# Layer change of a two-layer gated network: tile 2's parts taken from the PSUM banks, second products one block later, s*q+b on VectorE

## The chip, the cores and the metric

The kernel runs on one core of one Trainium2 chip. The metric is the device time of one execution in microseconds, median of three runs. Each core has TensorE (PE, matmuls, with the queue PEld for its weight loads), VectorE (DVE), ScalarE (ACT), GpSimd (POOL) and SyncE (SP, which issues the loads here).

## The reference

A retention layer gives 1536 tokens of 512 values. Two dense layers with 2048 hidden units follow. The change concerns the passage from the first to the second.

```python
def _moe_ref(x, w_in, w_out):          # first layer
    h = x @ w_in
    g = np.maximum(h, 0.0) + np.log1p(np.exp(-np.abs(h)))
    return (g @ w_out).astype(np.float32)

def _moe2_ref(x, w_in, w_out, s, b):   # second layer
    h = x @ w_in
    r = np.maximum(h, 0.0)
    g = s * (r * r) + b
    return (g @ w_out).astype(np.float32)
```

## The kernel before

**Tiles.** The 1536 tokens are three tiles of 512 (`j` = 0, 1, 2), the 512 values four chunks of 128 (`cc`). The activations of a tile stand in `xa[j]` as plain fp32 and, for the matmuls, as two parts: `xh` (rounded) and `xl` (what is left). A product with two parts on each side takes three matmuls, high by high, high by low, low by high, so a block of four chunks takes 12 matmuls of 512 columns. Weights are split in the same way: one 64-bit weight tile `raw` is turned into fp32 by two VectorE operations into `word` (L290, L292), a ScalarE copy into `wm` (L295) and a third VectorE operation (L300), and then into `wh` (ScalarE) and `wl` (GpSimd) by `split`, L110. `split_w` is a generator of these steps, and `go(work, n)` runs n of them.

**A block.** A first product gives a bank of hidden values: `h`, `y` or `third`. The activation function turns it into `c`, and `parts_g` splits `c` into `gh` (ScalarE) and `gl` (GpSimd). In the second layer the function is Relu (L559), Square (L584), and s*q+b as a ScalarE Identity with scale and bias (L585). The second products then add `gh`, `gl` times `w_out` into four sum banks (`acc01`, two banks in one tile, `acc2`, `acc3`); there is one set of them, so whoever comes next must wait until they are emptied into `xa` (`take_2`: in the first pair of the second layer a VectorE copy, L621; later an addition, L623).

**The change of layer.** The last steps of the first layer end with tile 2: `end` runs the second products of step `NS - 1`, `sum_last` adds the banks to `xa[2]` (L423), and `parts_last` makes `xh` (ScalarE, L428) and `xl` (VectorE, L430) of it. Meanwhile `plain(1, 0, ...)` runs the first pair of hidden blocks of the second layer: six blocks, `k` = 0 to 5, two for each tile. With each block goes an entry of `accs`: three of the old layer (`left`), then the two second products of tile 0 (`whole`), then nothing. From pair 1 on, `second` uses a scheme with fewer products, in which sums of the tiles (`sum_x` with x1 to x4, `sum_z`) replace the tiles; their sums and parts are made in the same stretch.

**What sets the order.** The order is written by hand: the code is issued as it stands, each engine works off its own queue in that order, and waits are set where one engine needs another's result. Between two engines there is no other order.

Of the kernel before, what the change touches and what calls it, by code (L numbers as in the profile page):

```python
# [7 lines left out]
F32 = mybir.dt.float32  # L8
F32R = mybir.dt.float32r
U32 = mybir.dt.uint32  # L10
AF = mybir.ActivationFunctionType
ALU = mybir.AluOpType
# [10 lines left out]
NTILE = NT // TT  # L23
CPT = TT // C
KC = DM // P
# [23 lines left out]
def tile_retention_mlps(ctx: ExitStack, tc: tile.TileContext, head, w1, w2, sb, out):  # L49
    nc = tc.nc  # L50
# [31 lines left out]
    sbt = cp.tile([P, 2], F32, tag="sbt", name="sbt")  # L82
# [335 lines left out]
    def sum_last(banks):  # L418

        la, g, j, _ = steps[NS - 1]  # L420
        for cc in banks:
            t = xa[j][:, cc]
            nc.vector.tensor_tensor(out=t, in0=acc_t[la, g, j][cc], in1=t, op=ALU.add)  # L423

    def parts_last():
        j = NTILE - 1
        for cc in range(KC):
            nc.scalar.activation(xh[j][:, cc], xa[j][:, cc], AF.Copy)  # L428
        for cc in range(KC):
            nc.vector.tensor_tensor(  # L430
                out=xl[j][:, cc], in0=xa[j][:, cc], in1=xh[j][:, cc].bitcast(F32), op=ALU.subtract
            )

    x_t, x3 = {}, {}

# [119 lines left out]
    def begin(la, src, own=False, by_pool=True, tags=None):  # L555

        if la:
            c = src if own else next_t()
            nc.scalar.activation(c, src, AF.Relu)  # L559
            return src, c, None  # L560
        if tags:
            r, u = (late.tile([P, TT], F32, tag=tag, name=tag) for tag in tags)
        else:
            r, u = next_t(), None
        if by_pool:
            nc.scalar.activation(r, src, AF.Relu)
            return src, r, u if tags else src if own else next_t()
        nc.vector.tensor_scalar(
            out=r.bitcast(U32), in0=src.bitcast(U32), scalar1=0x80000000, scalar2=None, op0=ALU.bitwise_or
        )  # L570
        nc.scalar.activation(r, r, AF.Softplus)
        return src, r, None

    def middle(of):

        src, r, u = of
        if u is not None:
            nc.vector.scalar_tensor_tensor(out=u, in0=r, scalar=-2.0, in1=src, op0=ALU.mult, op1=ALU.add)
            nc.scalar.activation(u, u, AF.Softplus)

    def finish(la, p, half, j, of):
        src, c, u = of
        if la:
            nc.scalar.activation(c, c, AF.Square)  # L584
            nc.scalar.activation(c, c, AF.Identity, scale=sbt[:, 0:1], bias=sbt[:, 1:2])  # L585
        elif u is not None:
            nc.gpsimd.tensor_tensor(out=c, in0=c, in1=u, op=ALU.add)  # L587
            late_parts.append((la, p, half, j, c))
            return
        else:  # L590
            nc.vector.scalar_tensor_tensor(out=c, in0=src, scalar=0.0, in1=c, op0=ALU.max, op1=ALU.add)
        parts_g(la, p, half, j, c)
# [3 lines left out]
    def parts_g(la, p, half, j, c):  # L596
        gg_t[la, p, half, j] = gh, gl = next_g()
        split(gh, gl, c, nc.scalar, nc.gpsimd)
# [29 lines left out]
    NS = len(steps)  # L628
# [54 lines left out]
    def go(work, n):  # L683
        for _ in range(n):
            next(work, None)
# [68 lines left out]
    with tc.manual_schedule():  # L754
# [149 lines left out]
        def end_part():  # L904
            while late_parts:
                parts_g(*late_parts.pop(0))
            go(late_work, 1)
# [34 lines left out]
        def of_pair(la, p, j, half):  # L942
            def take(banks):
                if half:
                    take_2(la, p, j, banks)

            return lambda banks: acc_2(la, p, j, half, banks), take

        def whole(acc, take):
            acc(FIRST + SECOND)  # L950
            take(FIRST + SECOND)

        def plain(la, p, left, sums, parts):

            w = la * NF + 2 * p
            base = at[la, p + 1]
            accs = left + [lambda: whole(*of_pair(la, p, 0, 0)), lambda: whole(*of_pair(la, p, 0, 1)), lambda: None]
            banks = [(ps_h, "h"), (ps_y, "y"), None, (ps_h, "h"), None, (ps_y, "y")]
            for k, (j, half) in enumerate((j, half) for j in range(NTILE) for half in range(2)):
                part(base + k + 2 if la or k > 1 else 0)  # L960
                to = bank(*banks[k]) if banks[k] else bank_2[1]
                all_of(to, w_t[w + half, 0], j)
                if la and k == 2:
                    end_part()
                    accs[k]()
                of = begin(la, to, by_pool=False)
                if not la:
                    end_part()
                    go(work, 2)
                finish(la, p, half, j, of)  # L970
                if la:
                    end_part()
                if not la or k != 2:
                    accs[k]()
                go(work, 3 if la else 1)
                for x in sums[k]:
                    next(x, None)
                for x in parts[k]:
                    parts_x(x, la)
# [286 lines left out]
```

## Time and profile before

| | us |
|---|---|
| median of three runs | 565.93 (565.83 to 566.22) |
| the profiled execution | 565.88 |
| its span | 564.0 |
| TensorE busy | 557.2 (99%) |
| VectorE busy | 383.7 (68%) |
| ScalarE busy | 349.4 (62%) |
| GpSimd busy | 348.9 (62%) |

Times of rows are microseconds from the span's start. A row of windows holds a stretch and its length, the busy time and (in brackets) the number of instructions of PE, PEld, DVE, ACT and POOL in this order, TensorE's granted clock as a share of full speed (1.00 is 2.4 GHz), the busy share of the DMA engines and GB/s. A matmul's record is 0.39 us long, but the next one starts 0.227 us later: the records overlap, so busy time hides gaps shorter than the overlap, and a wait is read from the starts. The same holds on ScalarE and VectorE, where one operation starts a little before the record of the one before it ends.

### The profile page before, as it was taken

How to read it: one execution, taken by the hardware profiler on the slowest of the kernel's cores; microseconds unless marked ns; L12 is line 12 of the kernel's file. 1: busy time of each engine (PE TensorE's matmuls, PEld its weight loads, DVE VectorE, ACT ScalarE, POOL GpSimd, SP SyncE). 2: the span in 40 equal slices, each digit the busy share in tenths (PEclk: the TensorE clock that was granted, in tenths of full speed). 3: DMA queues.
4: the chain of work that ended last, by engine and by line, in shares of the span. 5: the costliest groups of instructions: out<-in, count | busy, mean ns of one | idle time of the engine just before them, and what ended most of it. 6: DMA issues, size and time to landing. Idle time of an engine off the chain costs nothing.

```text
span 564.0 us, 8397 instructions
## 1 busy us (share of the span) xinstructions
PE 557.2 (99%) x3098; PEld 465.4 (83%) x3098; DVE 383.7 (68%) x581; ACT 349.4 (62%) x641; POOL 348.9 (62%) x293
## 2 busy tenths in 40 slices
PE   8999999999999999999999999999999999999997
PEld 7877888888888888888888777888888888888886
DVE  4887768776757759786859887675665665656334
ACT  3766673544554665543437878858687776868561
POOL 4457467776598797733525999647566555646230
PEclk9999999999999999999999999999999999999999
DMA  8986112101222213322212022222211221110005
GB/s 342 405 355 223 41 38 65 48 29 48 74 76 73 76 37 111 115 76 77 73 38 76 0 74 76 76 74 76 75 63 53 74 74 41 73 38 2 0 11 213
DMA packets 15016, 50.61 MB, mean 90 GB/s; under 512 B 1792, under 2 KB 2048, under 8 KB 14976
## 3 DMA queue, kind: packets, MB, share of 16 engines
q1 hardware_dynamic: 14976, 50.08, 25.1%
q8 instruction: 24, 0.39, 0.3%
q14 instruction: 16, 0.13, 0.1%
HBM read 46.93 MB, written 3.15 MB: 89 GB/s over the span
## 4 chain that ended last, share of the span: by engine, by line
PE 92%; POOL 4%; ACT 2%; DVE 1%; issue 1%; DVEq 0%
PE acc L613 33%; PE acc L403 11%; PE h L494 9%; PE y L494 8%; PE h L352 8%; PE third L494 5%; PE y L352 4%; PE y L502 3%; PE third L502 2%; PE y L191 2%; PE s L172 2%; PE h L502 1%; PE h L191 1%; POOL gl L115 1%; PE acc L775 1%
## 5 line engine op out<-in xcount | busy, mean ns | idle before, releaser
L115 POOL TENSOR_TENSOR wl<-wm,wh 128x512 fp32r<-128x512 f32 x64 | 84.6, 1322 | 101.0 <-ACT wh L112 101.0
L115 POOL TENSOR_TENSOR gl<-c,gh 128x512 fp32r<-128x512 f32 x69 | 91.0, 1324 | 70.3 <-ACT gh L112 48.5
L623 DVE TENSOR_TENSOR xa<-acc,xa 128x512 f32<-128x512 f32 x131 | 82.3, 683 | 71.4 <-PE acc L613 71.2
L613 PE MATMUL acc<-wh,gl 128*128 128x512 f32 x190 | 74.3, 391 | 0.0
L613 PE MATMUL acc<-wh,gh 128*128 128x512 f32 x190 | 74.1, 390 | 0.0
L613 PE MATMUL acc<-wl,gh 128*128 128x512 f32 x190 | 53.9, 390 | 0.0
L112 ACT ACTIVATE gh<-c 128x512 fp32r<-128x512 f32 x69 | 43.6, 632 | 10.9 <-POOL c L587 6.9
L295 ACT ACTIVATE wm<-raw 128x512 f32<-128x512 f32 x64 | 42.4, 663 | 8.7 <-POOL wl L115 8.6
L300 DVE SCALAR_TENSOR_TENSOR wm<-wm,cu,word 128x512 uint32<-128x512 uint32 x54 | 39.9, 739 | 4.1 <-ACT wm L295 3.4
L292 DVE SCALAR_TENSOR_TENSOR word<-raw,cu,word 128x512 uint32<-128x512 uint32 x54 | 40.8, 756 | 1.9
L613 PEld LDWEIGHTS acc<-wl,gh 128*128 128x128 f32 x190 | 35.7, 188 | 7.6
L112 ACT ACTIVATE wh<-wm 128x512 fp32r<-128x512 f32 x64 | 39.7, 620 | 3.2 <-DVE wm L300 3.0
L613 PEld LDWEIGHTS acc<-wh,gl 128*128 128x128 f32 x190 | 35.8, 188 | 6.6
L613 PEld LDWEIGHTS acc<-wh,gh 128*128 128x128 f32 x190 | 35.8, 188 | 6.4
L585 ACT ACTIVATE c<-c,sbt 128x512 f32<-128x512 f32 x48 | 39.2, 816 | 1.6
L365 ACT ACTIVATE t<-t 128x512 f32<-128x512 f32 x24 | 15.1, 629 | 38.9 <-DVE t L359 38.9
L403 PE MATMUL acc<-gh,wh 128*128 128x512 f32 x96 | 37.9, 395 | 0.0
L403 PE MATMUL acc<-gl,wh 128*128 128x512 f32 x96 | 37.4, 390 | 0.0
L613 PE MATMUL acc<-gh,wh 128*128 128x512 f32 x96 | 37.3, 389 | 0.0
L613 PE MATMUL acc<-gl,wh 128*128 128x512 f32 x96 | 37.3, 389 | 0.0
L290 DVE TENSOR_SCALAR word<-raw 128x512 uint32<-128x512 uint32 x54 | 37.0, 686 | 0.4
L559 ACT ACTIVATE c<-c 128x512 f32<-128x512 f32 x21 | 13.1, 633 | 33.6 <-DVE c L552 33.6
(265 smaller groups left out, 1461.4 us busy)
## 6 DMA issues: line engine op xcount, KB each, us to landing
raw<-w SPq DMA_DIRECT2D x64, 512.0 KB, 3.5
qk<-head SPq DMA_DIRECT2D x12, 512.0 KB, 8.3
kv<-head SPq DMA_DIRECT2D x12, 512.0 KB, 8.4
out<-xa SPq DMA_DIRECT2D x11, 256.0 KB, 2.1
cst<-head SPq DMA_DIRECT2D x1, 518.0 KB, 4.4
cst<-head SPq DMA_DIRECT2D x1, 256.0 KB, 5.4
out<-xa SPq DMA_DIRECT2D x2, 128.0 KB, 1.8
sbt<-sb SPq DMA_DIRECT2D x1, 1.0 KB, 10.3
```

The lines of the kernel that those rows point to most:

```text
L112: nc.scalar.activation(hi, src, AF.Copy)
L115: lo_eng.tensor_tensor(out=lo, in0=src, in1=hi.bitcast(F32), op=ALU.subtract)
L290: nc.vector.tensor_scalar(out=x, in0=lw, scalar1=29, scalar2=None, op0=ALU.logical_shift_right)
L292: nc.vector.scalar_tensor_tensor(out=x, in0=hw, scalar=cu[:, 0:1], in1=x, op0=ALU.bitwise_and, op1=ALU.bitwise_or)
L295: nc.scalar.activation(m, hw.bitcast(F32), AF.Copy, scale=REBIAS)
L300: nc.vector.scalar_tensor_tensor(out=m.bitcast(U32), in0=m.bitcast(U32), scalar=cu[:, 1:2], in1=x, op0=ALU.logical_shift_left, op1=ALU.bit ...
L352: nc.tensor.matmul(ps, w[:, cc * P : (cc + 1) * P], r[j][:, cc, :], start=i == 0, stop=i == len(ops) - 1)
L403: nc.tensor.matmul(acc_t[la, g, j][cc], *ops[i], start=f4 == 0 and i == 0, stop=ends(s) and i == 2)
L494: nc.tensor.matmul(ps, w[a][:, k * P : (k + 1) * P], x[b][:, k], start=start and i == 0, stop=i == len(ops) - 1, skip_group_check=True,)
L585: nc.scalar.activation(c, c, AF.Identity, scale=sbt[:, 0:1], bias=sbt[:, 1:2])
L613: nc.tensor.matmul(acc_t[la, p, "pair", j][cc], *ops[i], start=half == 0 and i == 0, stop=half == 1 and i == 2)
L623: nc.vector.tensor_tensor(out=dst, in0=ps, in1=dst, op=ALU.add)
```

## The change

Four things change, all at the change of layer, and nothing else in the program.

- `sum_last` adds `xa[2]` into the sum banks and leaves the result there; `parts_last` reads the banks, ScalarE for `xh`, VectorE for `xl`; a new `whole_last` copies the banks to `xa[2]` on ScalarE (four copies), after the Relu of block `k` = 2.
- In the second layer's first pair `accs` is now: three of the old layer, nothing, and then the two second products of tile 0. They go with blocks 4 and 5 instead of 3 and 4. The banks of blocks 4 and 5 are exchanged: block 4 goes to `y` and block 5 to `third`.
- In blocks 2 to 5 a new `squared` makes the Square on ScalarE and s*q+b as a VectorE tensor-scalar operation, both in place on `c`.
- In these blocks two steps of the weights (L290, L292 with the ScalarE copy, L300) come between `squared` and `parts_g`, so `gh` follows them.

```diff
         for cc in banks:
-            t = xa[j][:, cc]
-            nc.vector.tensor_tensor(out=t, in0=acc_t[la, g, j][cc], in1=t, op=ALU.add)
+            t = acc_t[la, g, j][cc]
+            nc.vector.tensor_tensor(out=t, in0=t, in1=xa[j][:, cc], op=ALU.add)
...
+        ps = acc_t[la, g, j]
         for cc in range(KC):
-            nc.scalar.activation(xh[j][:, cc], xa[j][:, cc], AF.Copy)
+            nc.scalar.activation(xh[j][:, cc], ps[cc], AF.Copy)
...
+            nc.vector.tensor_tensor(out=xl[j][:, cc], in0=ps[cc], in1=xh[j][:, cc].bitcast(F32), op=ALU.subtract)
+
+    def whole_last():
+        la, g, j, _ = steps[NS - 1]
+        for cc in range(KC):
+            nc.scalar.activation(xa[j][:, cc], acc_t[la, g, j][cc], AF.Copy)
...
+    def squared(c):
+        nc.scalar.activation(c, c, AF.Square)
+        nc.vector.tensor_scalar(
+            out=c, in0=c, scalar1=sbt[:, 0:1], scalar2=sbt[:, 1:2], op0=ALU.mult, op1=ALU.add
+        )
...
-            accs = left + [lambda: whole(*of_pair(la, p, 0, 0)), lambda: whole(*of_pair(la, p, 0, 1)), lambda: None]
+            own_accs = [lambda: whole(*of_pair(la, p, 0, 0)), lambda: whole(*of_pair(la, p, 0, 1))]
+            accs = left + ([lambda: None] + own_accs if la else own_accs + [lambda: None])
             banks = [(ps_h, "h"), (ps_y, "y"), None, (ps_h, "h"), None, (ps_y, "y")]
+            if la:
+                banks[4:] = banks[:3:-1]
...
                 of = begin(la, to, by_pool=False)
+                if la and k == 2:
+                    whole_last()
                 if not la:
                     end_part()
                     go(work, 2)
-                finish(la, p, half, j, of)
-                if la:
+                if la and k > 1:
+                    squared(of[1])
                     end_part()
+                    go(work, 2)
+                    parts_g(la, p, half, j, of[1])
+                    go(work, 1)
+                else:
+                    finish(la, p, half, j, of)
+                if la and k < 2:
+                    end_part()
+                    go(work, 3)
                 if not la or k != 2:
                     accs[k]()
-                go(work, 3 if la else 1)
+                if not la:
+                    go(work, 1)
```

What this does to the queues, at three places. VectorE from the last subtraction for `xl` on, before (`word` and `wm` are the weights' steps, `xa1<-xa0,xa1` is the sum for x4, `xa0<-acc` empties the sum banks, `xa2<-xa2` are the sums for z):

```order
L430 TENSOR_TENSOR xl2_108<-xa2_111,xh2_105 128x512 x4
L290 TENSOR_SCALAR word_1170<-raw_2878 128x512
L292 SCALAR_TENSOR_TENSOR word_1170<-raw_2878,cu_99,word_1170 128x512
L300 SCALAR_TENSOR_TENSOR wm_3226<-wm_3226,cu_99,word_1170 128x512
L448 TENSOR_TENSOR xa1_110<-xa0_109,xa1_110 128x1024
L621 COPY xa0_109<-acc01_3209 128x512 x2
L621 COPY xa0_109<-acc2_3210 128x512
L621 COPY xa0_109<-acc3_3211 128x512
L290 TENSOR_SCALAR word_1170<-raw_3005 128x512
L292 SCALAR_TENSOR_TENSOR word_1170<-raw_3005,cu_99,word_1170 128x512
L300 SCALAR_TENSOR_TENSOR wm_3279<-wm_3279,cu_99,word_1170 128x512
L538 TENSOR_TENSOR xa2_111<-xa2_111 128x2x256 x2
```

And of the change, from the sum for x4 on (the two first s*q+b and the first three weight operations stand ahead of it):

```order
L452 TENSOR_TENSOR xa1_110<-xa0_109,xa1_110 128x1024
L587 TENSOR_SCALAR c_3241<-c_3241,sbt_98 128x512
L290 TENSOR_SCALAR word_1170<-raw_3005 128x512
L292 SCALAR_TENSOR_TENSOR word_1170<-raw_3005,cu_99,word_1170 128x512
L300 SCALAR_TENSOR_TENSOR wm_3249<-wm_3249,cu_99,word_1170 128x512
L542 TENSOR_TENSOR xa2_111<-xa2_111 128x2x256 x2
L587 TENSOR_SCALAR c_3289<-c_3289,sbt_98 128x512
L290 TENSOR_SCALAR word_1170<-raw_3062 128x512
L292 SCALAR_TENSOR_TENSOR word_1170<-raw_3062,cu_99,word_1170 128x512
L300 SCALAR_TENSOR_TENSOR wm_3297<-wm_3297,cu_99,word_1170 128x512
L631 COPY xa0_109<-acc01_3260 128x512 x2
L631 COPY xa0_109<-acc2_3261 128x512
```

The copies that empty the sum banks move from just behind the sum for x4 to behind two s*q+b, two groups of weight operations and the sums for z.

ScalarE from the Relu of block 3 on, before (`c<-h` is that Relu, `x4h` the high part of x4, `c<-third` the Relu of block 4):

```order
L559 ACTIVATE c_3201<-h_3188 128x512
L584 ACTIVATE c_3201<-c_3201 128x512
L585 ACTIVATE c_3201<-c_3201,sbt_98 128x512
L112 ACTIVATE gh_3205<-c_3201 128x512
L295 ACTIVATE wm_3226<-raw_2878 128x512
L485 ACTIVATE x4h_3234<-xa1_110 128x1024
L559 ACTIVATE c_3251<-third_1171 128x512
L584 ACTIVATE c_3251<-c_3251 128x512
```

And of the change, from the same Relu to the Relu of block 5, which now reads `third`:

```order
L563 ACTIVATE c_3205<-h_3192 128x512
L586 ACTIVATE c_3205<-c_3205 128x512
L295 ACTIVATE wm_3211<-raw_2878 128x512
L112 ACTIVATE gh_3217<-c_3205 128x512
L489 ACTIVATE x4h_3223<-xa1_110 128x1024
L563 ACTIVATE c_3241<-y_3228 128x512
L586 ACTIVATE c_3241<-c_3241 128x512
L112 ACTIVATE wh1_3209<-wm_3211 128x512
L295 ACTIVATE wm_3249<-raw_3005 128x512
L112 ACTIVATE gh_3255<-c_3241 128x512
L563 ACTIVATE c_3289<-third_1171 128x512
```

The Identity is gone, each `gh` stands behind a weight copy, and `third` is read by the last of the six Relus instead of the last but one.

TensorE behind block 3's low matmuls, before (`acc01<-wh1,gh` begins the second products of tile 0):

```order
L502 MATMUL h_3188<-xl1_107,wh0_2733 128x512
L502 MATMUL h_3188<-xh1_104,wl0_2734 128x512 x4
L613 MATMUL acc01_3209<-wh1_2826,gh_3050 128x512
L613 MATMUL acc01_3209<-wh1_2826,gl_3051 128x512
L613 MATMUL acc01_3209<-wh1_2826,gh_3050 128x512
```

And of the change:

```order
L506 MATMUL h_3192<-xl1_107,wh0_2733 128x512
L506 MATMUL h_3192<-xh1_104,wl0_2734 128x512 x4
L506 MATMUL y_3228<-xh2_105,wh0_2673 128x512
L506 MATMUL y_3228<-xl2_108,wh0_2673 128x512
L506 MATMUL y_3228<-xh2_105,wh0_2673 128x512
```

Tile 2's first block stands directly behind block 3, one block earlier than before, and the second products of tile 0 come behind it, one block later.

## Rows read from the trace of the kernel before

**Rows 1.** Windows of two stretches (columns as told under time and profile).
```profile
333.00:341.00 8.00, 6.89 (x31) 5.39 (x30) 7.15 (x9) 5.58 (x10) 8.00 (x6) 1.00 0.41 133
...
350.00:560.00 210.00, 210.00 (x1067) 179.47 (x1066) 118.55 (x190) 150.25 (x256) 112.95 (x100) 1.00 0.17 59
```

**Rows 2.** Waits of TensorE: who, for whom, us in total, times, longest.
```profile
PE h L494 <- ACT p L508: 1.1, 1, 1.1
PE y L494 <- ACT p L508: 0.6, 1, 0.6
PE third L502 <- DVE xl L430: 0.4, 1, 0.4
```

**Rows 3.** Timeline of TensorE: start, length, line, operation [idle before and releaser].
```profile
316.58 0.39 PE L502 MATMUL h<-xh,wh 128*128 128x512 f32 x1
...
323.38 0.39 PE L502 MATMUL third<-xh,wh 128*128 128x512 f32 x1
324.18 0.50 PE L502 MATMUL third<-xl,wh 128*128 128x512 f32 x1 [0.41 <-DVE xl L430]
324.51 1.09 PE L502 MATMUL third<-xh,wl 128*128 128x512 f32 x4
...
337.23 0.61 PE L494 MATMUL y<-x1h,sl 128*128 128x512 f32 x2
338.96 0.50 PE L494 MATMUL h<-x2h,sh 128*128 128x512 f32 x1 [1.11 <-ACT p L508]
...
342.27 1.07 PE L613 MATMUL acc<-wl,gh 128*128 128x512 f32 x4
343.91 0.50 PE L494 MATMUL y<-xh,sh 128*128 128x512 f32 x1 [0.57 <-ACT p L508]
```

**Rows 4.** Timeline of VectorE, from tile 2's additions to the sums for z.
```profile
315.42 2.48 DVE L423 TENSOR_TENSOR xa<-acc,xa 128x512 f32<-128x512 f32 x4 [2.28 <-PE acc L403]
317.82 6.30 DVE L430 TENSOR_TENSOR xl<-xa,xh 128x512 fp32r<-128x512 f32 x4
324.04 0.68 DVE L290 TENSOR_SCALAR word<-raw 128x512 uint32<-128x512 uint32 x1
...
326.31 1.30 DVE L448 TENSOR_TENSOR xa<-xa,xa 128x1024 f32<-128x1024 f32 x1
327.91 2.48 DVE L621 COPY xa<-acc 128x512 f32<-128x512 f32 x4 [0.30 <-PE acc L613]
...
333.21 2.84 DVE L538 TENSOR_TENSOR xa<-xa 128x512 f32<-128x512 f32 x2
```

**Rows 5.** Timeline of ScalarE in the same stretch.
```profile
321.14 1.14 ACT L112 ACTIVATE sh<-ws 128x512 fp32r<-128x512 f32 x2
...
322.79 0.63 ACT L584 ACTIVATE c<-c 128x512 f32<-128x512 f32 x1
323.46 0.82 ACT L585 ACTIVATE c<-c,sbt 128x512 f32<-128x512 f32 x1
...
327.64 1.06 ACT L485 ACTIVATE x4h<-xa 128x1024 fp32r<-128x1024 f32 x1 [2.14 <-DVE xa L448]
328.61 0.58 ACT L559 ACTIVATE c<-third 128x512 f32<-128x512 f32 x1
...
343.28 0.57 ACT L508 ACTIVATE p<-y 128x512 f32<-128x512 f32 x1
343.76 0.58 ACT L508 ACTIVATE u<-h 128x512 f32<-128x512 f32 x1
```

**Rows 6.** Windows of the span's end.
```profile
560.50:561.00 0.50, 0.49 (x5) 0.29 (x3) 0.24 (x1) 0.00 (x0) 0.00 (x0) 1.00 1.00 369
...
562.50:563.00 0.50, 0.00 (x0) 0.00 (x0) 0.00 (x0) 0.00 (x0) 0.00 (x0) 1.00 0.48 160
563.00:563.50 0.50, 0.00 (x0) 0.00 (x0) 0.00 (x0) 0.00 (x0) 0.00 (x0) 0.78 0.00 0
563.50:564.00 0.50, 0.00 (x0) 0.00 (x0) 0.00 (x0) 0.00 (x0) 0.00 (x0) 0.50 0.00 0
```

More of the change, by code (lines that the diff above doesn't have):

```diff
@@ L421, in sum_last @@
         for cc in banks:
-            t = xa[j][:, cc]
-            nc.vector.tensor_tensor(out=t, in0=acc_t[la, g, j][cc], in1=t, op=ALU.add)
+            t = acc_t[la, g, j][cc]
+            nc.vector.tensor_tensor(out=t, in0=t, in1=xa[j][:, cc], op=ALU.add)
     def parts_last():
-        j = NTILE - 1
+        la, g, j, _ = steps[NS - 1]
+        ps = acc_t[la, g, j]
         for cc in range(KC):
-            nc.scalar.activation(xh[j][:, cc], xa[j][:, cc], AF.Copy)
+            nc.scalar.activation(xh[j][:, cc], ps[cc], AF.Copy)
         for cc in range(KC):
-            nc.vector.tensor_tensor(
-                out=xl[j][:, cc], in0=xa[j][:, cc], in1=xh[j][:, cc].bitcast(F32), op=ALU.subtract
-            )
+            nc.vector.tensor_tensor(out=xl[j][:, cc], in0=ps[cc], in1=xh[j][:, cc].bitcast(F32), op=ALU.subtract)
+    def whole_last():
+        la, g, j, _ = steps[NS - 1]
+        for cc in range(KC):
+            nc.scalar.activation(xa[j][:, cc], acc_t[la, g, j][cc], AF.Copy)
     x_t, x3 = {}, {}
```

## The prediction, made before the changed kernel was run

> **What bounds the kernel now.** I read the windows first: TensorE is busy for all 210 us of the stretch from 350 to 560, at full granted clock, so nothing that other engines do there can shorten the run; in the stretch from 333 to 341 it is busy for 6.89 of 8 us [rows 1]. So the stretch around the change of layer is the one to look at. The waits of TensorE name what it waited for there: once a VectorE part of tile 2, twice a ScalarE copy [rows 2]. The order in time gives their price [rows 3]. Matmuls of 512 columns follow each other every 0.227 us (12 of a block in 2.72). Between 323.38 and 324.18 lie 0.80 us, so 0.57 are lost; the last of the pair at 337.23 starts at 337.46 and the next at 338.96, 1.27 lost; the last of the four at 342.27 starts at 342.95 and the next at 343.91, 0.73 lost. After each wait one more gap is 0.33 instead of 0.23 (324.18 to 324.51), together 0.3. **All that can be won is 2.9 us.** After 350 us TensorE never waits, so a microsecond of TensorE wait more or less in this stretch is a microsecond of run time. The profiled execution took 565.88 us (span 564.0, 1.88 around it), the median of the runs is 565.93; I add to 565.88.
>
> **TensorE's demand after the change.** The block at 316.58 (fourth block) [rows 3] keeps its time. Without waits then come: tile 2's first block 319.30, the first second product 322.02, tile 2's second block 324.74, the other second product 327.46 to 330.18, and from the next pair six matmuls into `h` 330.18, six into `third` 331.54, and at 332.90 the second products of tile 1, which need the four sum banks that were filled until 330.18.
>
> **Tile 2's parts.** Today four subtractions with both inputs in SBUF, beside a busy GpSimd, take 6.30 us, 1.57 each; the four additions with one input in a bank take 2.48, that is 0.60 from one to the next and 0.68 long [rows 4]. The change gives the subtractions a bank as input, so I price them at 0.60. Added: the second addition writes the tile that the first wrote and waits for it, about 0.1. Additions 315.42 to 318.0; ScalarE's four halves start at 316.9, and reading banks it goes from one to the next in 0.48 [rows 5]; subtractions 318.0 to 320.5. TensorE asks for the last at 320.9. So the wait of 0.57 goes although the block comes 2.7 us earlier. This part does what it says.
>
> **ScalarE's new load.** Halves and the Relu of the third block end at 319.3; the four new copies of the sums to `xa` wait for the subtractions and take 4 x 0.48, to 321.25. What goes: four multiplications by s of 0.82 [rows 5], now VectorE's. Their cost alone is in balance; what is not is the order.
>
> **VectorE's queue, the term that decides.** VectorE works in order. Its four new s*q+b wait each for a ScalarE Square, and behind them in its queue stand the nine bit operations on weights, the sum for x4, two sums for z, and at the very end the copies that empty the sum banks for the second products at 332.90. Before, these copies stood ahead of the second and third group of bit operations and started at 327.91, as soon as TensorE had filled the banks [rows 4]. Prices: an s*q+b is seen nowhere; the nearest row is the VectorE tensor-scalar at 324.04, 0.68 long [rows 4], so 0.6 from start to start; below it half of that, above it 1.3 (the contended subtraction, less what its second input costs). I take 0.6. Bit operations: 324.04 to 326.31, some 2.2 for three. Sum for x4 1.30, z sums 2.84 with gaps (I take 2.7), two copies 0.60 + 0.68 [rows 4]. ScalarE: 0.52 from one SBUF operation to the next (two in 1.14), Square 0.63, x4h 0.97 to the next start, Relu 0.58 [rows 5].
> Step by step: Square of the third block 321.25 to 321.9; two `sh` and `gh` to 323.4; Relu of the fourth block 324.0; Square 324.65. VectorE idles from 320.5, save for the first s*q+b, until this second one at 324.7. Then bit operations 325.3 to 327.5, x4 sum to 328.8. ScalarE, idle since 326, takes x4h at 328.8, then Relu 329.8 and Square 330.4 to 331.0 of the fifth block, whose product has lain ready since 322.0. VectorE, idle since 328.8, does the third s*q+b at 331.05, bit operations to 333.85, z sums to 336.55, the fourth s*q+b to 337.15, bit operations to 339.35, two copies to 340.6.
> ScalarE after 331.0: wh, wm, gh (3 x 0.52), Relu of the sixth block to 333.1. This block lies in `third`, since the two last blocks' banks are exchanged, and TensorE wants `third` back at 331.54: **wait of 1.6**, then 1.36 of matmuls to 334.55. There it stops for the sum banks until 340.65: **wait of 6.1**. Together 7.7. What is late next: the copies of `h` and `y` that it waited for twice before are done by 338.8 and 346.7, wanted at 344.7 and 348.8, so those waits vanish; the later banks come in time. GpSimd, on which ScalarE's weight operation waited before, has some 2 us of slack in the new chain. The loads of SP that wait for these bit operations move by the same microseconds, and their tiles are wanted a whole pair later. Net 7.7 - 2.9 = +4.8.
>
> **The clock.** No wait of today moves the granted clock: it is 1.00 between 333 and 341 [rows 1]. But at the end, with the last matmuls issued before 561, it is still 1.00 until 563.0, a mean of 0.78 in the half microsecond after and then 0.50, that is 1.2 GHz [rows 6]: it fell some 2.3 us after TensorE went quiet. A quiet of 6.1 us is well over that, so I expect the fall, and matmuls at half pace when it resumes. No row shows a rise. If it takes as long as the fall, 2.3 us at half pace lose 1.15; if one block of twelve runs at half pace, 2.7. I take 1.7; the ends are 0 and 2.7.
> The Trainium skill (TensorE: Matmul & The Clock Gate, Part 1) says that the throttled state is the default and that activity releases it; by that rule the block behind the long wait would begin at 1.2 GHz. The trace agrees on the fall alone.
> **Sum: 565.88 - 2.9 + 7.7 + 1.7 = 572.4.**
>
> **Rivals.**
> (a) The same chain, but the clock stays up: 570.7. Chance 0.15.
> (b) s*q+b at half the price. Three of the four lie on the chain, 0.3 each, so the waits are 6.9: 571.6, or 569.9 without the clock's fall. Chance 0.15. The Trainium skill (VectorE: DVE Perf Modes, The perf-mode tier table) gives a tensor-scalar of fp32 from SBUF to SBUF twice the rate of one that touches PSUM; by it this would be the case, and no row here shows such an operation.
> (c) s*q+b at 1.3, slowed by GpSimd: three times 0.7 more, 2.2 to 2.3 with the ripple: 574.7. Chance 0.07.
> (d) The subtractions stay at 1.57 though one input lies in a bank. The last ends at 324.3: TensorE loses 3.4 in tile 2's first block, the copies, Squares and all behind them come 3.6 later: 576.0. Against it stands the additions' row, with GpSimd as busy. Chance 0.03.
> (e) Faster: VectorE never waits for a Square. Then its own work from 320.5 (four s*q+b 2.4, bit operations 6.6, sums 4.0, copies 1.3) ends at 334.8, with s*q+b at half at 333.6; TensorE loses 1.9 or 0.75 where it loses 2.9 now: 564.9 or 563.7. It decides from 334.6 on: banks free before that make the kernel faster by over 0.2%. For it: the copies of `xa` and the fewer ScalarE multiplications free some ScalarE time. Against: ScalarE's queue puts the Square of the fifth block behind x4h, and x4h behind VectorE's own bit operations, which the order fixes. Chance 0.06 for faster, 0.04 for within 0.2%.
>
> **How the numbers follow.** The forecast itself has 0.50. Cases (a) to (d) are all slower by more than 0.2% (1.1 us, about what a measurement of this kernel can tell): slower 0.90, same 0.04, faster 0.06. Range 569.3 to 574.8: from (b) without the clock's fall, a little under, to (c); outside lie (d), (e) and no change, 0.13.
>
> **What would show it.** Right: TensorE's waits after the change are led by one of some 6 us behind the VectorE copies of `xa` near 334 to 341, with one of 1 to 2 us behind a ScalarE Relu just before; no wait for `xl`; subtractions of 0.6 to 0.7; a granted clock under 1 behind the long wait. VectorE's own waits stand at s*q+b, some 1.5, 2.1 and 2.3 us, for ScalarE. Wrong: copies of `xa` that start near 330.2, or Squares that come before VectorE asks. A first wait for `xl` of 3 us would mean (d).

## The result, and the profile after

| | before | after |
|---|---|---|
| median, us | 566.02 (565.83 to 566.22, 4 runs) | 572.89 (572.56 to 573.92, 4 runs) |
| the profiled execution, its span | 565.88, 564.0 | 573.92, 572.1 |
| mean granted clock of the profiled execution | 0.999 | 0.991 |
| TensorE busy | 557.2 | 559.7 |
| VectorE busy | 383.7 | 381.5 |
| ScalarE busy | 349.4 | 347.6 |

The changed kernel takes 1.0124 times as long (95% interval 1.0107 to 1.0142): 6.9 us more by the medians, where 6.5 were forecast (572.4 against 565.88). The profiled execution is the slowest of its four; it is 8.0 us behind the profiled one of before. Both numbers are explained below.

First the windows of the two stretches that answer to [rows 1] (a row: stretch, length, busy time and count of PE, PEld, DVE, ACT, POOL, granted clock, DMA share, GB/s):

```profile
333.00:341.00 8.00, 1.66 (x6) 1.05 (x6) 7.82 (x10) 3.45 (x6) 6.72 (x5) 0.74 0.32 103
350.00:560.00 210.00, 210.00 (x1064) 179.43 (x1063) 119.86 (x192) 154.85 (x264) 115.67 (x102) 1.00 0.17 54
```

The long stretch is as it was: TensorE full, clock 1.00. All of the loss lies ahead of it. Between 333 and 341 TensorE is busy for 1.66 us where it was busy for 6.89, while VectorE has gone up to 7.82 of 8: the engine that waits and the engine that is waited for stand in one row. ScalarE, at 3.45, mostly waits too.

The waits of TensorE (who, for whom, us in total, times, longest) answer to [rows 2]:

```profile
PE acc L623 <- DVE xa L631: 6.3, 1, 6.3
...
PE third L498 <- ACT c L563: 1.4, 1, 1.4
```

None of the three waits of [rows 2] is left, and two new ones stand here. (A wait of 1.5 near the kernel's start is in the list of both kernels and is left out here.) Their place, in TensorE's timeline (start, length, line, operation, idle before and releaser), answers to [rows 3]:

```profile
331.05 0.61 PE L498 MATMUL h<-xh,wl 128*128 128x512 f32 x2
333.04 0.50 PE L498 MATMUL third<-xh,wh 128*128 128x512 f32 x1 [1.38 <-ACT c L563]
...
334.08 0.63 PE L498 MATMUL third<-xh,wl 128*128 128x512 f32 x2
341.00 0.79 PE L623 MATMUL acc<-wh,gh 128*128 128x512 f32 x1 [6.29 <-DVE xa L631]
341.59 0.63 PE L623 MATMUL acc<-wh,gl 128*128 128x512 f32 x1
...
344.58 1.91 PE L623 MATMUL acc<-wl,gh 128*128 128x512 f32 x4
346.29 0.63 PE L498 MATMUL y<-x1h,sh 128*128 128x512 f32 x1
```

Read from the starts, as in the prediction: the pair at 331.05 would have been followed at 331.50, and the next matmul starts at 333.04, 1.54 lost; the pair at 334.08 would have been followed at 334.53, and the next starts at 341.00, 6.47 lost. Then the length of a matmul's record tells the rest: 0.63 instead of 0.39, and the twelve second products take from 341.00 to 346.29, 5.29 us instead of 2.72.

VectorE's timeline, to be laid beside [rows 4]:

```profile
315.38 2.63 DVE L423 TENSOR_TENSOR acc<-acc,xa 128x512 f32<-128x512 f32 x4 [2.28 <-PE acc L403]
317.97 2.48 DVE L431 TENSOR_TENSOR xl<-acc,xh 128x512 fp32r<-128x512 f32 x4
321.91 0.56 DVE L587 TENSOR_SCALAR c<-c,sbt 128x512 f32<-128x512 f32 x1 [1.46 <-ACT c L586]
324.62 0.55 DVE L587 TENSOR_SCALAR c<-c,sbt 128x512 f32<-128x512 f32 x1 [2.15 <-ACT c L586]
...
327.36 1.29 DVE L452 TENSOR_TENSOR xa<-xa,xa 128x1024 f32<-128x1024 f32 x1
330.94 0.55 DVE L587 TENSOR_SCALAR c<-c,sbt 128x512 f32<-128x512 f32 x1 [2.28 <-ACT c L586]
...
333.67 2.42 DVE L542 TENSOR_TENSOR xa<-xa 128x512 f32<-128x512 f32 x2
336.02 1.48 DVE L587 TENSOR_SCALAR c<-c,sbt 128x512 f32<-128x512 f32 x1
...
339.67 2.48 DVE L631 COPY xa<-acc 128x512 f32<-128x512 f32 x4
```

The copies that empty the sum banks (last row) start at 339.67, where they started at 327.91. Three of the four s*q+b (L587) have an idle ahead of them of 1.46 to 2.28 us for a Square of ScalarE. And the fourth takes 1.48 where the three others take 0.55 or 0.56. GpSimd's timeline shows what it ran beside:

```profile
335.51 1.71 POOL L115 TENSOR_TENSOR wl<-wm,wh 128x512 fp32r<-128x512 f32 x1
```

This operation ends at 337.22, and the fourth s*q+b ends 0.28 us behind it, at 337.50. The last section comes back to this.

ScalarE in the same stretch, beside [rows 5]:

```profile
319.29 2.07 ACT L436 ACTIVATE xa<-acc 128x512 f32<-128x512 f32 x4
321.22 0.66 ACT L586 ACTIVATE c<-c 128x512 f32<-128x512 f32 x1
...
328.69 1.06 ACT L489 ACTIVATE x4h<-xa 128x1024 fp32r<-128x1024 f32 x1 [2.85 <-DVE xa L452]
329.66 0.58 ACT L563 ACTIVATE c<-y 128x512 f32<-128x512 f32 x1
330.27 0.63 ACT L586 ACTIVATE c<-c 128x512 f32<-128x512 f32 x1
```

Here the two engines hold each other: ScalarE idles 2.85 us for the sum that VectorE makes at 327.36, and VectorE then idles 2.28 us for the Square at 330.27, which stands behind x4h in ScalarE's queue.

Last the clock, in windows of 1 us around the long wait (beside [rows 6]):

```profile
336.00:337.00 1.00, 0.00 (x0) 0.00 (x0) 1.00 (x2) 0.00 (x0) 1.00 (x1) 0.95 0.00 0
337.00:338.00 1.00, 0.00 (x0) 0.00 (x0) 1.00 (x2) 0.46 (x1) 0.22 (x1) 0.50 0.00 0
...
346.00:347.00 1.00, 1.00 (x4) 0.81 (x3) 0.00 (x0) 0.49 (x1) 0.96 (x1) 0.50 0.00 0
347.00:348.00 1.00, 1.00 (x5) 0.77 (x5) 0.00 (x0) 0.00 (x0) 1.00 (x2) 0.93 0.00 0
```

It fell from 2.4 to 1.2 GHz near 336.9, 2.2 us after the last matmul's end, and rose near 347.1, 6.1 us after TensorE had begun again. 1.54 + 6.47 of waits, less the 2.9 of before, and some 2.9 of half pace (by the third experiment) make 8.0: the whole difference of the two profiled executions.

### The profile page after: what moved, and what is told of

Same layout as the page of the kernel before. It is cut to its first block, busy times and chain, and to the rows that moved or that the text cites. A ratio compares the mean times of both kernels' runs of the same rounds, so it can differ in the third digit from the quotient of the medians.

```text
span 572.1 us, 8402 instructions
## 1 busy us (share of the span) xinstructions
PE 559.7 (98%) x3098; PEld 467.2 (82%) x3098; DVE 381.5 (67%) x585; ACT 347.6 (61%) x641; POOL 346.7 (61%) x293
## 4 chain that ended last, share of the span: by engine, by line
PE 93%; DVE 3%; ACT 3%; DMA 1%; issue 0%; DVEq 0%
PE acc L623 34%; PE acc L403 11%; PE h L498 9%; PE y L498 8%; PE h L352 8%; PE third L498 5%; PE y L352 4%; PE third L506 3%; PE y L506 3%; PE y L191 2%; PE s L172 2%; PE h L506 1%; PE h L191 1%; DMA qk<-head 1%; PE acc L172 1%; PE acc L191 1%
## 5 line engine op out<-in xcount | busy, mean ns | idle before, releaser
L295 ACT ACTIVATE wm<-raw 128x512 f32<-128x512 f32 x64 | 42.5, 663 | 7.1 <-POOL wl L115 7.0
L292 DVE SCALAR_TENSOR_TENSOR word<-raw,cu,word 128x512 uint32<-128x512 uint32 x54 | 40.8, 756 | 1.9
L300 DVE SCALAR_TENSOR_TENSOR wm<-wm,cu,word 128x512 uint32<-128x512 uint32 x54 | 40.0, 740 | 3.1 <-ACT wm L295 2.2
L290 DVE TENSOR_SCALAR word<-raw 128x512 uint32<-128x512 uint32 x54 | 37.1, 687 | 0.4
L595 ACT ACTIVATE c<-c,sbt 128x512 f32<-128x512 f32 x44 | 36.0, 817 | 1.5
```

What stands on the lines that cost most here:

```text
L290: nc.vector.tensor_scalar(out=x, in0=lw, scalar1=29, scalar2=None, op0=ALU.logical_shift_right)
L292: nc.vector.scalar_tensor_tensor(out=x, in0=hw, scalar=cu[:, 0:1], in1=x, op0=ALU.bitwise_and, op1=ALU.bitwise_or)
L295: nc.scalar.activation(m, hw.bitcast(F32), AF.Copy, scale=REBIAS)
L300: nc.vector.scalar_tensor_tensor(out=m.bitcast(U32), in0=m.bitcast(U32), scalar=cu[:, 1:2], in1=x, op0=ALU.logical_shift_left, op1=ALU.bit ...
```

## The experiments

The theory to be tested: TensorE waits because the copies that empty the sum banks stand last in VectorE's queue, behind s*q+b and bit operations that themselves wait for ScalarE; a quiet of TensorE that is long enough costs the clock on top. Rivals: that the price of s*q+b itself is the matter; that ScalarE's four new copies are; that one part alone carries the loss. Line numbers in the rows are those of each experiment's own code.

**1. s*q+b back on ScalarE.**

```diff
-        nc.vector.tensor_scalar(
-            out=c, in0=c, scalar1=sbt[:, 0:1], scalar2=sbt[:, 1:2], op0=ALU.mult, op1=ALU.add
-        )
+        nc.scalar.activation(c, c, AF.Identity, scale=sbt[:, 0:1], bias=sbt[:, 1:2])
```

> The change with s*q+b put back on ScalarE (Identity), all else as changed: VectorE no longer waits for a Square. Theory (the place of the sum-bank copies at the end of VectorE's queue, behind weight operations that themselves wait for ScalarE): VectorE now waits for ScalarE's weight copies instead, TensorE's long wait behind the xa copies stays, some 4.5 us, with 2.6 us at third before it; 570 to 573 us. Rival (VectorE's in-order waits for the Squares are the whole cause): those waits vanish, the copies are done by 334, TensorE loses under 2 us in all; 564 to 566 us.

Measured: 572.59 (572.07 to 573.12), ratio 1.0118 (1.0092 to 1.0144). The waits of TensorE are shared out otherwise than in the changed kernel, and than expected (2.6 and 4.5):

```profile
PE third L498 <- ACT c L563: 3.4, 1, 3.4
PE acc L621 <- DVE xa L629: 2.7, 1, 2.7
```

and VectorE no longer waits for a Square; in the list of its own waits of the stretch from 300 to 360 another copy of ScalarE stands in its place:

```profile
DVE wm L300 <- ACT wm L295: 8.8, 3, 5.1
```

TensorE gets its banks at 340.51 instead of 341.00. So which engine multiplies by s is nearly without weight: VectorE's queue stops at the bit operations for ScalarE's weight copy instead of at s*q+b for its Square, and the copies of the banks stand behind the one as behind the other.

**2. The copies of the banks first.** In the fifth and sixth block the copies of `xa` go ahead of s*q+b and of the bit operations; all else stays as changed.

```diff
+                if la and k > 2:
+                    accs[k]()
...
-                if not la or k != 2:
+                if not la or k < 2:
                     accs[k]()
```

> The change with the second products of blocks 4 and 5, and so the xa copies on VectorE, issued ahead of the block's own s*q+b and weight operations. Theory: the copies come 2.8 us earlier in VectorE's queue but still behind the sums for z, so the long wait shrinks from 6.3 to some 3.2 us, the wait at third stays at 1.4; with the clock up 568.2 us, up to 571 if it falls. Rival (ScalarE's added copies and Squares alone set the end): the place in VectorE's queue does not matter, 572 to 573 us.

Measured: 568.06 (567.89 to 569.55), ratio 1.0044 (1.0032 to 1.0056). Waits of TensorE:

```profile
PE acc L623 <- DVE xa L631: 2.7, 1, 2.7
...
PE third L498 <- ACT c L563: 1.4, 1, 1.4
```

VectorE's timeline shows the copies and the fourth s*q+b with their places exchanged:

```profile
336.01 2.47 DVE L631 COPY xa<-acc 128x512 f32<-128x512 f32 x4
338.40 0.53 DVE L587 TENSOR_SCALAR c<-c,sbt 128x512 f32<-128x512 f32 x1
```

The copies start 3.7 us earlier and 4.8 of the 6.9 us are back, the clock's among them: TensorE was quiet for 2.7 us and in the profiled run the clock stayed at 1.00. (In three of the nine runs the mean clock was 0.996 or 0.997, and these took 1.1 to 1.5 us more than the median.) With the same operations, only their order in one queue is worth most of the loss. What is left is 2.3 us; by the timelines it comes from the waits ahead, for x4h and the Square behind it, which no experiment took out by themselves.

**3. The same wait without the clock's fall.** 22 matmuls whose product nobody reads fill most of the long wait.

```diff
+            if la and p == 1:
+                for _ in range(22):
+                    nc.tensor.matmul(other, ah[:, 0:P], xh[0][:, 0, :], start=True, stop=True, skip_group_check=True)
```

> The changed kernel with 22 matmuls of no use (into the free bank y) put on TensorE between the last matmuls into third and the long wait's end. Theory: no engine's order or wait changes, the second products resume near 341.0 us as before, but at 2.4 GHz: the 12 matmuls take 2.72 instead of 5.29 us and the next ones start at full pace, 2.9 us less, 570.0 us. Rival (the slow matmuls are hidden by other waits behind them, or the added matmuls disturb): 572.5 to 573.5 us.

Measured: 571.13 (571.02 to 571.32), ratio 1.009 (1.0069 to 1.011). TensorE's timeline (the useless matmuls are those into `y`):

```profile
334.43 5.17 PE L1029 MATMUL y<-xh,wh 128*128 128x512 f32 x22
340.96 0.50 PE L623 MATMUL acc<-wh,gh 128*128 128x512 f32 x1 [1.36 <-DVE xa L631]
341.30 0.40 PE L623 MATMUL acc<-wh,gl 128*128 128x512 f32 x1
```

The banks come at the same time, 340.96, but the matmuls behind are short, and the clock is 1.00 throughout. This takes the two causes apart: by the medians the waits cost 5.4 us (571.13 less 565.76 of the runs of before beside it) and the clock the other 1.5; against the profiled execution of the changed kernel it is 2.9 (span 572.1 less 569.2). The 570.0 that I had expected took this 2.9 from the median, so it came out 1.1 too low. The four runs of the changed kernel lie 1.4 us apart (mean clock 0.991 to 0.994), those of this experiment 0.3: the slower a run, the lower its mean clock, so the spread is the clock's; the fifth experiment shows an earlier rise in another run.

**4. The exchange of the two banks undone.**

```diff
-            if la:
-                banks[4:] = banks[:3:-1]
```

> The change without the exchange of the banks of blocks 4 and 5 (third again for block 4, y for block 5). Theory: the wait of 1.4 us at third vanishes, but the one behind the xa copies grows by the same, since VectorE's queue sets its end: resume near 341.0 us, 572.5 to 573.2 us. Rival (the waits add up, each has its own cause): 571.3 us or less.

Measured: 573.28 (572.54 to 573.75), ratio 1.0126 (1.0104 to 1.0149). One wait of TensorE is left where there were two:

```profile
PE acc L623 <- DVE xa L631: 7.6, 1, 7.6
```

It ends at 340.91. The waits stand in series: what TensorE doesn't lose at `third` it loses at the sum banks, since VectorE's chain ends when it ends. The wait at `third` costs nothing as long as the other one is behind it.

**5. Without ScalarE's four new copies.**

```diff
-                if la and k == 2:
-                    whole_last()
```

> The changed kernel without ScalarE's four copies of the sums to xa[2] (so the sums for z are made of old values; it leaves that part of the computation out). Theory: ScalarE's queue starts the chain Square, s*q+b, weight operations, Square and so on 1.9 us earlier, every link moves with it: the wait at third vanishes, the copies come near 339.1 instead of 341.0; 1.9 us less and the clock still falls, 570.5 to 571.5 us. Rival (the copies themselves are what the change pays): most of the loss goes, 567 us or less.

Measured: 572.89 (572.22 to 573.48), ratio 1.0126 (1.0111 to 1.0142). (The sums for z are made of old values here; this kernel leaves that part of the computation out.) I had expected some 1.9 us less, and nothing came. VectorE's timeline shows where it went:

```profile
329.58 1.67 DVE L587 TENSOR_SCALAR c<-c,sbt 128x512 f32<-128x512 f32 x1 [2.28 <-ACT c L586]
```

and GpSimd's what it ran beside (two operations in one row, of which the first ends at 330.97):

```profile
329.68 2.72 POOL L492 TENSOR_TENSOR x4l<-xa,x4h 128x512 fp32r<-128x512 f32 x2
```

ScalarE is earlier, and so the third s*q+b starts at 329.58 instead of 330.94; but it takes 1.67 instead of 0.55 and ends at 331.25, 0.28 us behind that GpSimd operation, and the copies of the banks start at 339.44 instead of 339.67. That the four copies are the cause falls by this. That the chain's start is passed on to its end, which my expectation took for granted, falls too: the price of s*q+b depends on where GpSimd stands when it begins. The clock in this run, in windows:

```profile
343.00:344.00 1.00, 1.00 (x4) 0.79 (x3) 0.96 (x3) 1.00 (x3) 0.23 (x1) 0.63 0.07 16
344.00:345.00 1.00, 1.00 (x6) 0.79 (x5) 0.96 (x2) 0.97 (x2) 1.00 (x1) 1.00 0.00 0
```

After a wait as long (6.7 us) and a start again at 340.77, it is back near 343.7, after 3.0 us and not 6.1: half of that time is lost, 1.5 or 3.0, which are the two prices of the third experiment.

**6, 7 and 9. The parts one by one.** Three kernels leave two sets of parts out. The sixth has only tile 2's parts from the banks; the seventh has the new order of the four blocks too (s*q+b on VectorE, `gh` behind the weight steps), but not the later second products; the ninth has the later second products and the exchanged banks in the old order of blocks. Sixth and seventh:

```diff
-            accs = left + ([lambda: None] + own_accs if la else own_accs + [lambda: None])
+            accs = left + own_accs + [lambda: None]
...
-            if la:
-                banks[4:] = banks[:3:-1]
```

and, in the sixth and the ninth:

```diff
-                if la and k > 1:
-                    squared(of[1])
...
-                    go(work, 2)
-                    parts_g(la, p, half, j, of[1])
-                    go(work, 1)
-                else:
-                    finish(la, p, half, j, of)
+                finish(la, p, half, j, of)
...
-                if not la:
-                    go(work, 1)
+                go(work, 3 if la else 1)
```

> Before with tile 2's parts from the banks alone (and the copies to xa[2] that this needs); second products, s*q+b and the order of gh as before. Theory: the subtractions take 2.5 instead of 6.3 us and the wait for xl goes, but the second products of tile 0 wait some 1.1 us for the banks that ScalarE now empties later, and the two waits for copies of h and y stay or grow by ScalarE's 1.9 us: 566 to 568 us. Rival (this part alone brings the 0.6 us of the wait for xl): 565.2 us.

> The change without its second part: second products of tile 0 with blocks 3 and 4 and the banks as before; parts from the banks, s*q+b on VectorE and gh after the weights stay. Theory: the xa copies stand one block earlier in VectorE's queue, so the wait of 6.3 us breaks into short ones (for the banks 1.1 and 0.8, for copies of h and y 1.9 and 1.3), none long enough for the clock: 567.5 to 569.5 us. Rival (s*q+b on VectorE sets the end wherever the copies stand): 571 us or more.

> Parts from the banks, the later second products and the exchange of the two banks stay; the four blocks go back to the order and operations of before (ScalarE's Identity for s*q+b, the copies of xa ahead of the block's bit operations). Theory: the loss of the change comes from moving the second products a block later, since the copies that empty their banks then stand behind the whole of the fourth and fifth block in VectorE's queue, with or without the new block order; the copies start a little earlier than in the changed kernel (no s*q+b and only the earlier blocks' bit operations ahead of them), so TensorE loses some 6 us instead of 7.8: 570 to 571.5, about 570.8, with a longest wait of TensorE of 3 to 5 us and one of 1 to 3 us at the exchanged bank. Rival: the new block order is what makes the later second products dear; then this kernel stays near the one without the late products, 566 to 567.5, and no wait of TensorE is over 2 us.

Medians, with the ratio to before and its interval:

| | second products as before | a block later, banks exchanged |
|---|---|---|
| blocks in the old order | sixth: 566.39, 1.0007 (0.9998 to 1.0016) | ninth: 570.05, 1.0075 (1.0053 to 1.0097) |
| blocks in the new order | seventh: 567.22, 1.0026 (1.0017 to 1.0035) | changed kernel: 572.89, 1.0124 (1.0107 to 1.0142) |

The step to the right costs 3.7 and 5.7 us, the step down 0.8 and 2.8. The later second products carry most of the loss, in either order, and the new order makes it worse. That the new order is what makes them dear, the rival of the ninth, falls. The exchange of the banks was undone by itself in the new order alone (fourth experiment); in the old one it is not taken apart from the later second products. The seventh came 0.3 us below what I had expected. In the ninth the time was as expected (570 to 571.5), the way to it not. TensorE's waits were

```profile
PE third L498 <- ACT c L563: 3.3, 1, 3.3
PE acc L623 <- DVE xa L631: 0.6, 1, 0.6
```

with the long wait at `third`, and together 3.9 us where some 6 were expected. VectorE's idle in its list of waits (`DVE wm L300 <- ACT wm L295`, 10.3 us in three, the longest 5.9) is that of the first experiment. The rest is the clock: it fell in the wait at `third`, and TensorE, which began again at 334.90, ran at half pace until near 344.5. Two runs had a mean clock of 0.991 and took 571.2 and 571.3 us, the two others 0.997 and 568.9; the median in the table lies between the two pairs, which are 2.3 us apart.

The sixth is the same as before or 0.6 us slower. One of its waits shows why the parts from the banks bring nothing where the second products stay early:

```profile
PE acc L623 <- ACT xa L436: 1.0, 1, 1.0
```

The banks of tile 2's sums are read until ScalarE's four copies are through, and TensorE wants one of them before. The wait for `xl` is gone, one of 1.0 has come.

**10. Each s*q+b as two operations**, to measure what an operation more on the chain costs.

```diff
-        nc.vector.tensor_scalar(
-            out=c, in0=c, scalar1=sbt[:, 0:1], scalar2=sbt[:, 1:2], op0=ALU.mult, op1=ALU.add
-        )
+        nc.vector.tensor_scalar(out=c, in0=c, scalar1=sbt[:, 0:1], scalar2=None, op0=ALU.mult)
+        nc.vector.tensor_scalar(out=c, in0=c, scalar1=sbt[:, 1:2], scalar2=None, op0=ALU.add)
```

> The changed kernel with each of the four s*q+b split in two VectorE operations (a multiplication by s, then an addition of b). Theory: the second, third and fourth of them lie on the chain that ends with the copies of xa, so each added operation of some 0.5 us comes through: about 1.5 us more, 574.0 to 575.0, TensorE resumes its second products near 342.5 instead of 341.0, and the wait at third grows by some 0.5 (the second s*q+b alone lies ahead of it). The first has 2 us of slack and adds nothing. Rival: ScalarE's Squares and Relus set the chain and VectorE's operation is hidden in its waits; then nothing is added, 572.5 to 573.3.

Measured: 576.74 (576.03 to 577.26), ratio 1.0196 (1.0179 to 1.0213): 3.9 us more than the changed kernel, where I had expected 1.5. That nothing is added falls; the size was wrong by more than twice. TensorE's wait at `third` grew to 5.2 us, and it got its banks at 344.54, not near 342.5. VectorE's timeline:

```profile
321.74 0.58 DVE L587 TENSOR_SCALAR c<-c,sbt 128x512 f32<-128x512 f32 x1 [1.46 <-ACT c L586]
322.35 1.40 DVE L588 TENSOR_SCALAR c<-c,sbt 128x512 f32<-128x512 f32 x1
325.61 0.85 DVE L587 TENSOR_SCALAR c<-c,sbt 128x512 f32<-128x512 f32 x1 [1.85 <-ACT c L586]
326.49 1.40 DVE L588 TENSOR_SCALAR c<-c,sbt 128x512 f32<-128x512 f32 x1
...
339.03 1.49 DVE L587 TENSOR_SCALAR c<-c,sbt 128x512 f32<-128x512 f32 x1
340.56 0.48 DVE L588 TENSOR_SCALAR c<-c,sbt 128x512 f32<-128x512 f32 x1
```

and GpSimd's beside it:

```profile
320.72 2.75 POOL L492 TENSOR_TENSOR x2l<-xa,x2h 128x512 fp32r<-128x512 f32 x2
...
326.13 1.48 POOL L115 TENSOR_TENSOR gl<-c,gh 128x512 fp32r<-128x512 f32 x1
...
338.48 1.76 POOL L115 TENSOR_TENSOR wl<-wm,wh 128x512 fp32r<-128x512 f32 x1 [0.65 <-ACT wh L112]
341.78 1.27 POOL L115 TENSOR_TENSOR gl<-c,gh 128x512 fp32r<-128x512 f32 x1 [1.54 <-ACT gh L112]
```

Two things were wrong in my expectation. The added operation takes 1.4 and not 0.5 while GpSimd works: the one at 326.49 ends at 327.89, again 0.28 us behind GpSimd's operation (327.61). Only the last, at 340.56, when GpSimd was idle (from 340.24 to 341.78), takes 0.48. And the first s*q+b has no slack: its second half ends at 323.75, ScalarE's `gh` waits for it, and Relu and Square of the next block stand behind `gh`, so that the next s*q+b comes 1.0 us later (325.61 against 324.62).

**8. The order put right.** The experiments so far say what to keep: the parts from the banks and the later second products, but with nothing ahead of the bank copies that waits for ScalarE. So tile 2's copies to `xa` go from ScalarE to VectorE, s*q+b goes back to ScalarE, the copies of the banks and a z sum go ahead, bit operations are pulled ahead of the Relu in the last three blocks, and the banks aren't exchanged.

```diff
-            nc.scalar.activation(xa[j][:, cc], acc_t[la, g, j][cc], AF.Copy)
+            nc.vector.tensor_copy(xa[j][:, cc], acc_t[la, g, j][cc])
...
+                    if k > 2:
+                        go(work, 2)
+                    of = begin(la, to, by_pool=False)
...
+                    if k > 2:
+                        accs[k]()
+                    if k == 5:
+                        next(sums[5][0])
```

> Parts from the banks and later second products kept, the queues put in another order: copies to xa[2] on VectorE, s*q+b on ScalarE, the weights' ScalarE copies ahead of the Relu in blocks 3 to 5, xa copies and sums for z ahead of the block's weight operations, banks of blocks 4 and 5 as before. Theory (order of the queues, not the work in them): all long waits go, some 0.8 us remain of today's 2.9: 563.7 to 565 us, faster than before. Rival (the work added for the banks costs as much as the subtractions save): 565.5 to 568 us.

Measured: 564.91 (564.71 to 565.27, 11 runs), before beside it 565.83, ratio 0.9984 (0.9975 to 0.9993): faster than both kernels, than the one of before by 0.9 us. What TensorE still waits for here:

```profile
PE h L498 <- ACT p L512: 0.6, 1, 0.6
PE y L498 <- ACT p L512: 0.5, 1, 0.5
```

These are two of the three waits of [rows 2], each shorter; the copies of the banks start at 330.85 in VectorE's timeline. So the idea of the change holds 0.9 of the 2.9 us that [rows 3] had to give, if the copies keep their place.

## Why the prediction was right

Time, sign and mechanism were as forecast. Step by step, in the order of the prediction:

- **What bounds.** That a microsecond of TensorE's wait here is one of run time: the stretch from 350 to 560 is as full as before, and the starts of TensorE account for the 8.0 us.
- **Tile 2's parts.** Subtractions at 0.60 each, 318.0 to 320.5: 317.97, four in 2.48, no wait for `xl`. Rival (d) is out. That this part brings nothing by itself (sixth experiment) was not forecast.
- **ScalarE's new load**, to 321.25: its next Square starts at 321.22.
- **VectorE's queue.** Forecast and trace: second s*q+b 324.7 and 324.62; x4h 328.8 and 328.69; third s*q+b 331.05 and 330.94; z sums 333.85 and 333.67; fourth s*q+b 336.55 and 336.02; copies of the banks 339.35 and 339.67; TensorE's banks 340.65 and 341.00. The step that decided is thus shown, and the second experiment shows it by its removal.
- **The price of s*q+b** was taken as one value, 0.6, with 0.3 and 1.3 as ends. It has no single one: it took 0.46 or 0.47 from start to start for the second and third and 1.41 for the fourth, which began early in an operation of GpSimd. The sum of the three on the chain, 2.34, is 0.5 over the 1.8 of the forecast, and that little only because the values lie on either side of it; the z sums, at 2.35 instead of 2.7, gave back most of the difference. That the size was met is luck: the forecast gave s*q+b one price and had GpSimd only in rival (c).
- **The waits.** 1.54 and 6.47 lost against 1.6 and 6.1; less the 2.9, 5.1 against 4.8. They are in series, as the fourth experiment shows, so the split between them carries nothing.
- **The clock.** That it falls was right, and so was when: 2.2 us after the last matmul's end, where 2.3 had been read. The price was 1.7 with 0 and 2.7 as ends; measured 1.5 by the medians, 2.9 in the profiled execution, a little above the end. That the median met 1.7 is luck as well: the rise, after 6.1 us here and after 3.0 in the fifth experiment, is the size that was missing, and no row of before showed it. The Trainium skill's rule (TensorE: Matmul & The Clock Gate, Part 1), that activity must release a throttled state, is borne out by it: the second products began at 1.2 GHz.
- **Rivals.** (a) falls with the windows (0.50 behind the wait). (b) falls as a time: start to start, the second and third lie halfway between 0.3 and 0.6, but the fourth took 1.41. The Trainium skill's doubled rate for fp32 from SBUF to SBUF (VectorE: DVE Perf Modes, The perf-mode tier table) is seen only as a start-to-start of 0.46 against 0.60 for a copy from a bank. (c), slowed by GpSimd, is right in its mechanism for the fourth and out as a time. (e) falls: VectorE did wait for the Squares, by 1.5, 2.1 and 2.3 us as said.

A first reading of the change might blame s*q+b on VectorE, since it is the part that one sees; the first experiment speaks against that, and the ninth shows the later second products losing 4.2 us without it.

## What to carry to other kernels

VectorE worked off its queue in order here, so the copies at 339.67 waited for all that stood ahead of them: ahead of an operation that gives a resource back (here copies that empty sum banks) nothing should stand that waits for another engine, and before a consumer is moved to a later place one asks where the release of its buffer stands in its engine's queue. Two engines that each wait for the other's last result, as ScalarE for the x4 sum and VectorE for the Square behind it, make their waits add up. Here the order of one queue was worth 4.8 us; taking 1.9 us of ScalarE's copies out ahead of the chain gave nothing, because a third engine's operations held one link in place, and an operation more in each link cost 3.9. So a link is priced beside whatever else runs there. A wait of TensorE has a second price once it is long enough for the granted clock to fall; fill it or cut it in two and look at the clock of the windows behind it.

## What the runs showed of the hardware that I had not expected

- **The same tensor-scalar takes 0.48 to 0.58 us or 0.83 to 1.67, and it goes by GpSimd.** (128x512 fp32, SBUF to SBUF, on VectorE; 32 of them in the changed kernel and six experiments.) The three that ran with GpSimd idle took 0.48 (at 340.56 in the tenth), 0.53 and 0.54 (the fourth s*q+b of the second and the seventh). All twelve of 0.83 and more ended 0.28 or 0.29 us after the end of a GpSimd operation that ran beside them: 337.50 after 337.22 in the changed kernel, 331.25 after 330.97 in the fifth, 327.89 after 327.61 and 340.52 after 340.24 in the tenth. The other seventeen, 0.49 to 0.58, began 0.16 to 0.29 us before the end of GpSimd's operation, so that little of it was left to wait for. The one at 329.58 in the fifth began 0.14 us before the end of one and ended behind the next. A GpSimd operation that begins while a short one runs takes 1.47 to 1.56 instead of about 1.29. The Trainium skill (SBUF — State Buffer, section "SBUF: two separate sides") has a rule for this: the two engines share a pair of ports under an exclusive lock, and the one that comes second is blocked for the other's whole instruction. The trace agrees, with the 0.28 us above; that the ports are the cause is the page's account, no run here took them apart.
- **A subtraction with one operand in a bank doesn't feel GpSimd, and GpSimd doesn't feel it:** 0.60 instead of 1.57 each, with GpSimd busy in both; two of GpSimd's operations beside it (`x3l`) took 1.29 and 1.28 instead of 1.76 and 1.74.
- **The clock's rise isn't a fixed time.** It came 6.1 us after TensorE began again in one run and 3.0 in another, with the same work behind the wait; in the ninth experiment 9.6 us after, with a pause of 0.6 in between. Nor is the fall: 2.2 us after the last matmul in the changed kernel, 2.8 in the fifth experiment.
